# Phase tables of an S4 convolution: step tiles without doubled values, mode pairs written 128 bytes apart

## The chip, the cores and the metric

The kernel runs on one core of a Trainium2 chip. The core has five engines with queues of their own: TensorE (PE in the profile; its weight loads are the row PEld), VectorE (DVE), ScalarE (ACT), GpSimd (POOL) and SyncE (SP), which here only issues transfers. The metric is the device time of one execution in microseconds (us). The kernel before took 761.42 us in the median of three runs (760.34 to 763.97).

## The reference

The input is layer-normalised, and two branches are added to it: an S4 layer (a long convolution whose kernel K is a sum over 256 complex modes for each of 448 channels) and a PEER layer (16 heads, each picks the best of 64 x 64 experts by two scores, and adds a weighted row of a table).

```python
xn = layernorm(x)
# S4: K[d,l] = Re sum_n C[d,n] * dt*B[d,n] * exp(dt*A[d,n] * l),  l = 0..2047
P = exp((dt * A)[:, :, None] * l)
K = einsum("dn,dnl,dn->dl", C, P, dt * B).real
y = irfft(rfft(pad(xn)) * rfft(pad(K)))[:2048] + xn * Dskip
# PEER: q = xn @ w_q; s1, s2 = q1 . k1, q2 . k2; one expert per head
e = argmax(s1) * 64 + argmax(s2)
out = sum_h softmax(top) * gelu(xn . u[e]) * v[e]
result = x + y + out
```

The softmax is over one value.

## The kernel before, in words

**Convolution.** The 448 channels are cut into 56 batches of 8 (`batch`), two batches form a pair. A batch has R = 32 modes per partition (2 halves `h` of M = 16, which is 2 blocks of 128 modes times 8 channels). The exponential is split into magnitude and phase. TensorE makes the logarithms of the magnitudes (L579, L581) and ScalarE their exponentials `mg` (L590, L592). The phases are 32-bit integers, a full turn being 2 to the power 32, so sums wrap by themselves. For each mode 32 multiples a = 0..31 of the phase are needed. VectorE builds them in the tile `ph` for both batches of a pair by doubling: a first row (L610), then four additions (L614), which each add a shifted step to all that is there and so double it. The shifted steps are in the tile `st`, made by `steps` once for four batches by two shifts (L547) from the loaded phases `tp` and the shift amounts `amt`.

ScalarE turns the phases of one batch into a table `CS` with a sine half and a cosine half: sine (L629), absolute value (L632), and a sine of pi/2 minus that (L635). `CS` is ordered by mode, and within a mode by a: a mode's 32 values are contiguous. VectorE multiplies it into the magnitudes (L660, L662, L664, L666), TensorE sums over modes (L682), and after a small correction (L690, L693) transforms (L702) and ScalarE writes the result to `VK` (L706). After every 16 batches (the last time 8) `conv` multiplies with the transformed input: TensorE L798 (in the last piece L762 and L779), VectorE L808 (last piece L786), TensorE L830 (last piece L825), ScalarE L837, and SyncE stores the tile (L842). `final` loads it again (L1149, with a constant, L1151), transforms (L1159), copies (L1163), and GpSimd's queue adds it to the output (L1167).

**How phases lie before.** In `ph` the innermost index x (0 or 1) is the lowest bit of a. So two consecutive a of a mode are adjacent, 8 bytes. To add a step to both, `st` holds every step twice. ScalarE reads pairs: two values, then a jump of 512 bytes to the next pair. It writes `CS` without a gap.

**Scores and experts.** TensorE makes the scores (L961, L970), VectorE and ScalarE reduce them (L985 to L1006), and the indices go through memory. For the experts GpSimd's queue gathers rows (L1083), VectorE multiplies and sums each with the input (L1091), small steps on ScalarE and VectorE follow (L1098 to L1114), TensorE adds the weighted rows (L1121), ScalarE copies them (L1133), GpSimd's queue adds them to the output (L1136).

**Order.** Nothing is scheduled on the chip. `Plan` holds 72 streams of steps (`s4_ph` builds phases, `s4_act` the tables, `st_v` the shifted steps, `e_d` the experts' products and so on), and the string `ORDER`, one character a step, says whose next step is issued. Each engine executes its instructions in that order and waits by semaphores. The costs given with the steps in the code serve a planner outside and change nothing in the issued program.

Of the kernel before, what the change touches and what calls it, by code (L numbers as in the profile page):

```python
# [25 lines left out]
M = 2 * NB  # L26
# [89 lines left out]
class Plan:  # L116
# [57 lines left out]
    "4HH4HH44441444Z4444H606HH414144114H72III2II72II2I2I7728I8I2IJJ22I2I2I2I72KIZ414I82852I24K4I4COP224C4234LMLDHMHHH4LMDCLM4"  # L174
    "D3EC4EC6D44EI7II7IJJKKCLFDECMFDDEFF77877I47CI7I999FD9EEL44I7CCE8MFD8FDI749x48EI4F87CEC57IDD4N4FFRCRE9I47I79ZL4CFEFDR4EA4"
    "D7CF4MZ4xIENC979F8D8LIDEQ7SFI7M6EN7SRFARR7SOPSRQAA99JZSZAAGcGcSRSTRRSSRROdPSSRaBHUUUUxSUSSTUUUUUUUUUVWWeRRHXNYSSSaRYRRgS"
    "HbyyQfSOHyPRSLRSTyJhMRhgLhhgfRhhMffIfyhUzSSUzIUyGzRURSxz!S#!hUhI#yIzS$IyyQyO$Ih%ySiPcSTzyzUzURhzUyhy!##HURIU!HzI$U$zUR%S"
    "zUIygU!#ISh!h#yyyISRzKRVROizWx$W$%yyfziHHhNgxSfSzxPxKLISiz!#JM#RjRLRSfI!$$%QzIhhgTJfiIziGISSzMfykI!#yIyU#RUi&hRhh!yI$S$i"
    "dIeRXUSzUO%jhSIUNSlizIIhPkhLRhQzISMLhTMyRdiLzibURe!yyRzMfUzlyUiU##NY!U$$%LShSgJRjyRZZSifMhKhgHzz!UzKxiHfSfaN#Ufyy(LJ!Skh"
    "M#$hOPgUzxUiSL$%RRSyhhyymzxHTMhmlizxUUSRhhhn!nhHjhkhgLMURiUSLhhUyz#gRyRQV1iziSIiNI!fiIzz!ifSYclmISfhM#fQ$I$%hnSSgO#IyTWf"  # L180
    "IiUzjhiKZPhHI!&hRmUIhR#QkW$UhnI$UyyyyUzIzlzU%!hHjRy#z!iziS#Iy$RS$hkJyyyL%ZiUSzzHHdMhyRyLMelIbROzISz!I#!Iy#$SygiPfIhiSSXm"
    "zfzhRJmRUfRU$%L!nITnjhgfi#SIUIfMLhIhMkUIUiSgRRR#h!ISli$$N%OIJjKxcNJhzxyyVhhcyyxSzzSyUySUxzSzh!TPi#h!h#QmULUWZ$aih&Kyyhnf"
    "$UfURfU%MRziSzUgyzyLhNMhRgifSLfRQz!hSiH(yhg#HWzz#h!$R$hhbjZzz%Riyh!k#y!#MHYO$SSd$%iyHPIhekSizIIUSzlliIiRRLjhIKQghTzIUiSh"
    "UIR!#UihISMkhKyIyyfI!UI#URlmyS$I$fURfSShnJVY%NcgROhKxhfSajXxUizzyyPiSxzgLkhyymRQixzz!M#z#N!$Rhym$lhzfinyL&%RTSyzy(njUSUz"
    "hUz!yhhgzhzMU#Uhk!!SWR##il$$fh!Ri%R#hzhJfyi$yzfyxz$OzyfgxSxxS%KfimSiSiUhhP!gL#RMRhjhL#TiUiyUWSd!z$hRUSyzRMR$yy%yhkhSiyhS"
    "izUnjzhkilSROUNY(Qzlh!zhSzUPy&#!y#ymiSR$z$egyUb%hny!h#!aRyzTizfzUgzSfyyRURSXfiUR#$NQSU$UROzUihSSxoz!xYhgmzSf%yzSyP#h#Uy!"
    "h!hyfURRjnhTiRkhhS$U#hyS$y%UiymjUzilk!#UlxV$$xg%&hzzz!zzWh#!(Sn#hRSyyzyiz!iyyRmRS#V#$Wh!my$$inno$fUoyfigSSph%hzfgp%zfzUq"
    "rzqzyyphYj!hhzUrizfiyTkqpqroz#rhhhi#!!dpjqlW#$hrebiUh#kst$!hpg%pqWhxh$iorfoo$qltUxpgypyfzrhqxhciXfUg%irszijhUyifq&pzfrUi"
    "yhkhyyxy(zlzU!thozy#p#!qzz$hy$pjq!hr##iy!z$cay%yhhiyg$yUzfyUhzfqhrzhkpz%qr!pyyygUVzrtWihhuqppl#zfzyghrfi#!hy!ms(#fd#$yqm"
    "hyu!hr$%nqteth$ii$irnyiymjYbxxmhxsihnkxKnhjii%tzhWilgfhhYt&ykzgzzQffzzzz!yhhgh#if#yy!l$fmmh!$#h#!izz%iji$ynhyyuhnhyzkhhl"  # L190
    "z$zzihjgfhzi!hf#z!kayfli#gfifib$ih!hg$mhhuhijd%#hi)heh)(ym!nini#*ki$ljhxzXm%i+hhkf$xzxlxngh%hmgyyyizzifi&f!ynhhjgyy#yyhh"
    "i!khflf#zh$h*$y+hjmnkhca%hzziiilmnYyzg!hiz#y!hhzzyf#$zjgh$chzfykg%yh!zfzfifihdhzl#!hmi#i!eh##nh)o*+jb$i$!i$hg$ihk,%%ix)x"
# [12 lines left out]
class Kernel:  # L205
# [22 lines left out]
    def alloc(s):  # L228
# [1002 lines left out]
```

## Time and profile before

| | |
|---|---|
| median of three runs | 761.42 us |
| the profiled execution, its own time | 763.02 us |
| its span from first to last instruction | 761.1 us |
| VectorE busy | 669.5 us, 88% |
| TensorE busy | 652.1 us, 86% |
| ScalarE busy | 552.9 us, 73% |
| GpSimd busy | 360.7 us, 47% |
| mean granted TensorE clock | 0.915 |

The profile is one execution. A page gives each engine's busy time, a strip of 40 equal slices (a digit is the busy share in tenths) and groups of instructions: line, engine, operation, output and input tile, shape, count, busy time and mean length, then the idle time of the engine ahead of them and what ended it. Other views of the same trace cut it into stretches, list who waited for whom, and follow the chain of work that ended last.

### The profile page before, as it was taken

The numbers are of one execution on the slowest core, as the hardware profiler recorded it, in microseconds if no ns is written. First come the engines' busy times: TensorE is split into PE (matmuls) and PEld (weight loads), VectorE is DVE, ScalarE is ACT, GpSimd is POOL, SyncE is SP. The second block draws the span as 40 slices with busy tenths as digits, with TensorE's granted clock in tenths as the row PEclk, the third lists the DMA queues.
The fourth block names the chain that finished last, engine by engine and source line by source line (L and its number), as shares of the span: only waits on it lengthen the run. The fifth ranks groups of instructions, "written<-read, shape, count | busy, mean of one in ns | idle before, by whom it ended". The sixth has DMA issues, their size and how long they took to land.

```text
span 761.1 us, 19861 instructions
## 1 busy us (share of the span) xinstructions
PE 652.1 (86%) x7628; PEld 355.8 (47%) x7628; DVE 669.5 (88%) x1691; ACT 552.9 (73%) x1137; POOL 360.7 (47%) x307
## 2 busy tenths in 40 slices
PE   1999999999999999999887958679996587899882
PEld 0344333443444444444465734346763344576751
DVE  4896578999999999999999999999998999999840
ACT  3886147566876886774796898888898888999630
POOL 2011024544363645655447686484564657752523
PEclk9999999999999999999999877688987756999995
DMA  9998656978687896887989999899898999977998
GB/s 324 328 374 305 228 136 254 355 238 246 221 257 266 252 327 191 309 255 257 337 300 340 281 324 361 263 327 279 265 342 271 308 325 286 339 248 209 296 178 128
DMA packets 119095, 211.83 MB, mean 278 GB/s; under 512 B 38937, under 2 KB 94233, under 8 KB 118937
## 3 DMA queue, kind: packets, MB, share of 16 engines
q0 software_dynamic: 31232, 124.80, 51.6%
q1 hardware_dynamic: 87768, 85.77, 35.2%
q8 instruction: 60, 0.98, 0.5%
q14 instruction: 35, 0.28, 0.1%
HBM read 180.90 MB, written 33.29 MB: 281 GB/s over the span
## 4 chain that ended last, share of the span: by engine, by line
PE 41%; DVE 29%; ACT 14%; DMA 7%; issue 6%; SPq 1%; POOL 1%; POOLq 0%; DVEq 0%; ACTq 0%
PE sc L961 14%; DVE ue L1091 6%; PE U L798 3%; PE po L1121 3%; DVE mg L666 3%; DVE zi L662 3%; DVE ph L614 3%; PE kp L682 3%; PE sc L970 3%; DMA ue<-in_uv_dram,ig 3%; PE ip L830 2%; PE wc L862 2%; PE up L724 2%; ACT CS L629 2%; DMA VU<-vu_d 2%
## 5 line engine op out<-in xcount | busy, mean ns | idle before, releaser
L1083 POOL DMA_INDIRECT ue<-in_uv_dram,ig x256 | 312.6, 1221 | 309.0 <-PE po L1121 72.9
L961 PE MATMUL sc<-W,xt 128*128 128x512 f32 x384 | 180.1, 608 | 2.2 <-ACT xt L946 1.9
L1091 DVE SCALAR_TENSOR_TENSOR ue<-ue,xr 128x448 f32<-128x448 f32 x256 | 154.1, 617 | 4.0 <-DMA ue<-in_uv_dram,ig 4.0
L961 PEld LDWEIGHTS sc<-W,xt 128*128 128x128 f32 x384 | 69.7, 191 | 91.9 <-issue 83.9
L1121 PE MATMUL po<-ue,A 128*32 128x448 f32 x512 | 68.6, 616 | 9.4 <-DVE A L1114 5.0
L590 ACT ACTIVATE mg<-lg 128x512 f32<-128x512 f32 x112 | 63.4, 600 | 11.1 <-PE lg L579 10.6
L682 PE MATMUL kp<-mg 128*32 128x64 f32 x1792 | 62.3, 237 | 7.9 <-DVE kt L693 3.1
L666 DVE TENSOR_TENSOR mg<-mg,CS 128x1024 f32<-128x1024 f32 x56 | 68.2, 1217 | 0.0
L662 DVE TENSOR_TENSOR zi<-mg,CS 128x1024 f32<-128x1024 f32 x56 | 68.2, 1217 | 0.0
L635 ACT ACTIVATE CS<-CS,halfpi 128x1024 f32<-128x1024 f32 x56 | 64.5, 1152 | 0.8
L614 DVE CUSTOM_DVE_ANT_0 ph<-st,ph 128x512 uint16<-128x512 uint16 (+2 forms) x84 | 64.9, 772 | 0.2
L629 ACT ACTIVATE CS<-ph 128x1024 f32<-128x1024 int32 x56 | 62.6, 1118 | 1.4 <-issue 0.5
L632 ACT ACTIVATE CS<-ph 128x1024 f32<-128x1024 int32 x56 | 63.2, 1128 | 0.0
L682 PE MATMUL kp<-zi 128*32 128x64 f32 x1792 | 61.6, 234 | 0.0
L682 PEld LDWEIGHTS kp<-mg 128*32 128x32 f32 x1792 | 45.2, 119 | 29.2 <-issue 11.7
L579 PE MATMUL lg<-lc,rt 32*128 32x512 f32 x112 | 39.8, 548 | 21.5 <-ACT mg L590 17.5
L702 PE MATMUL vp<-f,kt 128*64 128x128 f32 x448 | 43.6, 326 | 16.5 <-ACT tl L1163 5.0
L985 DVE TENSOR_REDUCE mx<-sc 128x8 f32<-128x512 f32 x64 | 43.6, 682 | 14.6 <-PE sc L970 9.2
L682 PEld LDWEIGHTS kp<-zi 128*32 128x32 f32 x1792 | 47.2, 121 | 0.1
L798 PE MATMUL U<-VU,g 128*64 128x128 f32 x384 | 42.3, 301 | 5.4 <-DVE cp L808 2.7
L702 PEld LDWEIGHTS vp<-f,kt 128*64 128x64 f32 x448 | 28.9, 160 | 38.3 <-issue 11.9
L862 PE MATMUL wc<-wq,kk 128*64 128x448 f32 x128 | 31.7, 586 | 17.1 <-DMA wq<-in_wq_dram 17.1
(244 smaller groups left out, 1242.2 us busy)
## 6 DMA issues: line engine op xcount, KB each, us to landing
wq<-in_wq_dram SPq DMA_DIRECT2D x32, 448.0 KB
xr<-xn_d SPq DMA_DIRECT2D x64, 224.0 KB
vu_d<-vst SPq DMA_DIRECT2D x64, 112.0 KB
VU<-vu_d SPq DMA_DIRECT2D x12, 512.0 KB
t_d<-tq SPq DMA_DIRECT2D x24, 256.0 KB
tl<-t_d SPq DMA_DIRECT2D x12, 512.0 KB
ue<-in_uv_dram,ig POOLq DMA_INDIRECT x256, 6.4
xx<-in_x_dram SPq DMA_DIRECT2D x16, 224.0 KB
```

The costliest lines, as they stand in the source:

```text
L614: s.nc.vector.tensor_tensor(out=rw(n, 2 * n), in0=rw(0, n), in1=o["st"][:, k, b0:b0 + 2].rearrange("p b h m x -> p (b h m x)")[:, None].to ...
L629: s.nc.scalar.activation(CS[:, 1].rearrange("p (m r x) -> p m r x", r=16, x=2), four(s.ph), AF.Sin, scale=SC)
L635: s.nc.scalar.activation(B["CS"][:, 0], B["CS"][:, 0], AF.Sin, scale=-SC, bias=s.halfpi)
L662: V.tensor_tensor(out=zi[:, 512:], in0=mg[:, 512:], in1=CS[:, 1], op=ALU.mult)
L666: V.tensor_tensor(out=mg[:, 512:], in0=mg[:, 512:], in1=CS[:, 0], op=ALU.mult)
L682: s.nc.tensor.matmul(kp[32 * c:32 * c + 32, 64 * gi:64 * gi + 64], T[ri][:, 1024 + m:1056 + m], view(T[ri], m, [[512, 2], [1, 32]]), start ...
L702: s.nc.tensor.matmul(vp[64 * ri:64 * ri + 64, 128 * gi:128 * gi + 128], B["kt"][:, 64 * gi:64 * gi + 64], s.f1[:, ri], start=True, stop=True)
L798: s.nc.tensor.matmul(U[64 * h:64 * h + 64, sl, ri], s.g[q][:, 2 * kk + h, ri], src[:, k1 + h, :w], start=True, stop=True)
L961: s.nc.tensor.matmul(B["sc", q].rearrange("p a b -> p (a b)"), B["xt"][:, i], w, start=(q % 2 == 0 and i == 0), stop=(q % 2 == 1 and i == 2))
L1083: s.nc.gpsimd.indirect_dma_start(out=ue, out_offset=None, in_=s.io["uv"], in_offset=bass.IndirectOffsetOnAxis(ap=s.IDX[t][:, c, g:g + 1].b ...
L1091: s.nc.vector.scalar_tensor_tensor(Q["ue", c][:, :D], Q["ue", c][:, :D], 1.0, B["xr", c], op0=ALU.mult, op1=ALU.mult, accum_out=Q["dot"][: ...
L1121: s.nc.tensor.matmul(B["po"][32 * c:32 * c + 32, :D], Q["A"][:, c], Q["ue", c][:, D:], start=(g == 0), stop=(g == 3))
```

## The change

Three things change.

1. `st` holds each step once: the two shifts write 256 values a partition each and not 512. `amt` is transposed to suit.
2. In `ph` x now stands outside batch, half and mode, so that two adjacent values are two modes of one a. The first row is copied by x and no longer by h, each of its two instructions writing 64 contiguous values; the four additions have the sizes they had, and the added step row of 64 values is repeated 2, 4, 8 and 16 times in place of a row of 128 repeated 1, 2, 4 and 8 times. ScalarE's L629 and L632 read pairs of modes, with a jump of 256 bytes from pair to pair, and write the two modes of a pair 128 bytes (32 values) apart. `CS` holds the same values in the same places as before, so nothing behind it changes.
3. `ORDER` is a new string of the same steps. As many instructions of each kind are issued as before, with two exceptions: ScalarE's table loads are 64 in place of 62, and the shapes named above. The lines behind `steps` lie 1 to 4 lower in the file (L786 before is L782 after, L1091 is L1087).

```diff
 ORDER = (
-    "4HH4HH44441444Z4444H606HH414144114H72III2II72II2I2I7728I8I2IJJ22I2I2I2I72KIZ414I82852I24K4I4COP224C4234LMLDHMHHH4LMDCLM4"
...
+    "4HH4HH4474441464447I22II26442242I42IIC2447I1I4DI44012IC2I4I781HHJ414OECDC85FHH2JD8P274E8E4FLID7IIMF7IC2D22I4I44IECLCMID7"
...
-        s.amt = c.tile([128, 2, 4], I32, name="amt")
-        s.ph = c.tile([128, 16, 2, 2, M, 2], I32, name="ph")
+        s.amt = c.tile([128, 4, 2], I32, name="amt")
+        s.ph = c.tile([128, 16, 2, 2, 2 * M], I32, name="ph")
...
-            o["st"] = s.sm.tile([128, 4, 4, 2, M, 2], I32, name="st", bufs=s.o["ST"])
+            o["st"] = s.sm.tile([128, 4, 4, 2, M], I32, name="st", bufs=s.o["ST"])
             for h in range(2):
-                a = s.amt[:, h]
-                s.nc.vector.tensor_tensor(out=view(o["st"], 2 * M * h, [[16 * M, 4], [4 * M, 4], [1, 2 * M]]),
-                                          in0=view(o["tp"][:, 0, 0], 0, [[0, 4], [1, 4 * M], [0, 2]]),
-                                          in1=view(a, 0, [[1, 4], [0, 8 * M]]), op=ALU.logical_shift_left)
+                s.nc.vector.tensor_tensor(out=o["st"][:, :, :, h], in0=view(o["tp"][:, 0, 0], 0, [[0, 4], [M, 4], [1, M]]),
+                                          in1=view(s.amt, h, [[2, 4], [0, 4], [0, M]]), op=ALU.logical_shift_left)
...
                 if k < 0:
-                    for h in range(2):
-                        s.nc.vector.tensor_scalar(s.ph[:, 0, :, h].rearrange("p b m x -> p x b m"), o["tp"][:, :, h, b0:b0 + 2], 0, None,
-                                                  op0=ALU.logical_shift_left)
+                    for x in range(2):
+                        s.nc.vector.tensor_scalar(s.ph[:, 0, x].rearrange("p b (h m) -> p b h m", h=2), o["tp"][:, x, :, b0:b0 + 2].rearrange("p h b m -> p b h m"),
+                                                  0, None, op0=ALU.logical_shift_left)
                 else:
-                    n = 1 << k
-                    s.nc.vector.tensor_tensor(out=rw(n, 2 * n), in0=rw(0, n),
-                                              in1=o["st"][:, k, b0:b0 + 2].rearrange("p b h m x -> p (b h m x)")[:, None].to_broadcast([128, n, 4 * R]),
-                                              op=ALU.add)
+                    n = 2 << k
+                    s.nc.vector.tensor_tensor(out=ph[:, n:2 * n], in0=ph[:, :n],
+                                              in1=o["st"][:, k, b0:b0 + 2].rearrange("p b h m -> p (b h m)")[:, None].to_broadcast([128, n, 2 * R]), op=ALU.add)
...
         def four(v):
-            return view(v.rearrange("p r b h m x -> p (r b h m x)"), 2 * R * (b % 2), [[2, R], [4 * R, 16], [1, 2]])
+            return view(v.rearrange("p r x b m -> p (r x b m)"), R * (b % 2), [[2, M], [2 * R, 32], [1, 2]])
...
-            s.nc.scalar.activation(CS[:, 1].rearrange("p (m r x) -> p m r x", r=16, x=2), four(s.ph), AF.Sin, scale=SC)
+            s.nc.scalar.activation(CS[:, 1].rearrange("p (m c a) -> p m a c", a=32, c=2), four(s.ph), AF.Sin, scale=SC)
...
-            s.nc.scalar.activation(B["CS"][:, 0].rearrange("p (m r x) -> p m r x", r=16, x=2), four(s.ph), AF.Abs)
+            s.nc.scalar.activation(B["CS"][:, 0].rearrange("p (m c a) -> p m a c", a=32, c=2), four(s.ph), AF.Abs)
```

**What the new string does at three places.** The first is the end of VectorE's list, from the last product of the convolution on (`cp`, L786 before). `ue,dot` is an expert's product, `x`, `dw` and `th` are small steps of 4 values a partition, `A` the weights for TensorE. Before:

```order
L786 TENSOR_TENSOR cp<-us_8718,U 128x512
L1101 SCALAR_TENSOR_TENSOR x_8912<-x_8912,dot 128x4
L1114 TENSOR_TENSOR A<-mask,th 128x128
L1110 TENSOR_TENSOR dw<-dot,ig 128x4
L1107 SCALAR_TENSOR_TENSOR th<-th,dw 128x4
L1114 TENSOR_TENSOR A<-mask,th 128x128
```

Now, from the last `cp` (the third of a row of three) on:

```order
L782 TENSOR_TENSOR cp<-us_8694,U 128x512 x3
L1097 SCALAR_TENSOR_TENSOR x_8768<-x_8768,dot 128x4
L1103 SCALAR_TENSOR_TENSOR th<-th,dw 128x4
L1106 TENSOR_TENSOR dw<-dot,ig 128x4
L1110 TENSOR_TENSOR A<-mask,th 128x128
L1087 SCALAR_TENSOR_TENSOR ue,dot<-ue,xr 128x448
L1103 SCALAR_TENSOR_TENSOR th<-th,dw 128x4
L1087 SCALAR_TENSOR_TENSOR ue,dot<-ue,xr 128x448
L1110 TENSOR_TENSOR A<-mask,th 128x128
L1087 SCALAR_TENSOR_TENSOR ue,dot<-ue,xr 128x448 x2
L1097 SCALAR_TENSOR_TENSOR x_8978<-x_8978,dot 128x4
L1106 TENSOR_TENSOR dw<-dot,ig 128x4
```

after which a `th` and an `A` end the list. Four expert products that stood ahead of the convolution's last product now stand behind it.

The second place is TensorE's list at the same point. `ip` is the convolution's last transform (L825), `po<-ue,A` adds expert rows, `po<-tl,hl` is the work of `final`. Before:

```order
L825 MATMUL ip<-cp,e 128x256 x8
L1121 MATMUL po<-ue,A 32x448 x4
L825 MATMUL ip<-cp,e 128x256 x8
L1159 MATMUL po_8995<-tl,hl 32x128 x16
L1121 MATMUL po<-ue,A 32x448 x8
L1159 MATMUL po_9043<-tl,hl 32x128 x16
```

Now:

```order
L821 MATMUL ip<-cp,e 128x256 x8
L1155 MATMUL po_8983<-tl,hl 32x128 x16
L1117 MATMUL po<-ue,A 32x448 x12
L1155 MATMUL po_9039<-tl,hl 32x128 x16
L1155 MATMUL po_9066<-tl,hl 32x64 x16
```

The last transform no longer has expert rows ahead of it; all three remaining groups of them come behind.

The third place is ScalarE's list at the second and third pair of tables, where the two additional table loads are. Now (`exg` is an exponential for the experts, `th` a tanh):

```order
L1037 ACT_TABLE_LOAD
L1037 ACTIVATE exg<-top 128x32
L992 ACTIVATE eq<-sc,mx 128x64 x8
L723 ACTIVATE vst<-up 128x448
L686 ACTIVATE kt<-kp 128x2x63
L1094 ACTIVATE x_1210<-dot 128x4
L921 ACTIVATE xx<-xx,q,y 128x448
L625 ACT_TABLE_LOAD
L625 ACTIVATE CS<-ph 128x16x32x2
L1100 ACT_TABLE_LOAD
L1100 ACTIVATE th<-x_1210 128x4
L628 ACTIVATE CS<-ph 128x16x32x2
```

Before, the comparable stretch had one load ahead of both tables of a pair:

```order
L639 ACT_TABLE_LOAD
L639 ACTIVATE dum<-one 128x1
L1098 ACTIVATE x_948<-dot 128x4
L1104 ACTIVATE th<-x_948 128x4
L629 ACTIVATE CS<-ph 128x1024
L632 ACTIVATE CS<-ph 128x1024
L635 ACTIVATE CS<-CS,halfpi 128x1024
L946 ACTIVATE xt<-xtp 128x512
```

The exponential and the tanh now stand between the steps of a pair's tables and bring loads of their own.

More of the change, by code (lines that the diff above doesn't have):

```diff
@@ L178 @@
[L178 to L189, printed above, removed]
@@ L205 @@
+    "stt!#!$#)u$z$*z,+%,uu$z)%z!##!$$%&+(*,+))*)*)++**,,++,,,")
 class Kernel:
@@ L287, in sets @@
                 for k in range(4):
-                    s.nc.gpsimd.memset(s.amt[:, h, k:k + 1], k + 2 + 6 * h)
+                    s.nc.gpsimd.memset(s.amt[:, k, h:h + 1], k + 2 + 6 * h)
         x0 = s.amt_done = p.add("c_g", "POOL", 1600, sets)
@@ L543, in sh @@
         def sh():
[L544 removed]
+            o["st"] = s.sm.tile([128, 4, 4, 2, M], I32, name="st", bufs=s.o["ST"])
             for h in range(2):
[L546 to L549 removed]
+                s.nc.vector.tensor_tensor(out=o["st"][:, :, :, h], in0=view(o["tp"][:, 0, 0], 0, [[0, 4], [M, 4], [1, M]]),
+                                          in1=view(s.amt, h, [[2, 4], [0, 4], [0, M]]), op=ALU.logical_shift_left)
         x = p.add("st_ld", "SP", xf(512, 256), l, deps=s.tp_done, take=("tpl",))
[L551 removed]
+        o["ready"] = [p.add("st_v", "DVE", dv(512), sh, n=1, deps=[x, s.amt_done], take=("st",))]
         return o
```

47 lines of the change are left out of this document (28 added, 19 removed).

## The prediction

> **What bounds the kernel now.** I read the page's busy shares first, then the same cut into stretches, then who VectorE waits for, then the rows of the edited lines, and last the chain at the end.
>
> ```profile
> PE 652.1 (86%) x7628; PEld 355.8 (47%) x7628; DVE 669.5 (88%) x1691; ACT 552.9 (73%) x1137; POOL 360.7 (47%) x307
> core 0: us, PE busy (x) PEld busy (x) DVE busy (x) ACT busy (x) POOL busy (x), PEclk, DMA share, GB/s
> 0.00:375.00 375.00, 349.53 (x2270) 148.18 (x2270) 331.26 (x838) 247.44 (x571) 147.47 (x136) 1.00 0.81 274
> 375.00:700.00 325.00, 262.49 (x4428) 176.98 (x4430) 310.82 (x782) 281.89 (x513) 189.29 (x153) 0.84 0.94 299
> 700.00:730.00 30.00, 27.47 (x690) 22.27 (x684) 26.62 (x70) 18.34 (x43) 14.11 (x11) 1.00 0.78 222
> 730.00:761.00 31.00, 12.59 (x248) 8.36 (x246) 0.75 (x5) 5.23 (x13) 9.86 (x8) 0.68 0.99 174
> ```
>
> The cut at 375 us is where the scores end. Until then TensorE is the fullest engine (349.5 of 375 us). From 375 to 700 it is VectorE: 310.8 of 325 us, 96%; ScalarE follows with 281.9, that is with 43.1 us idle. From 730 on VectorE has nothing left and a tail of 31 us runs through transfers. So a microsecond less on VectorE behind 375 us should come off the end, while ScalarE has some room, but not much.
>
> ```profile
> DVE x L1101 <- ACT x L1098: 4.6, 6, 2.7
> DVE th L1107 <- ACT th L1104: 3.8, 5, 1.3
> ...
> DVE ue L1091 <- DMA ue<-in_uv_dram,ig: 2.0, 2, 1.0
> ...
> DVE zi L660 <- ACT CS L629: 1.3, 1, 1.3
> ```
>
> These are VectorE's waits from 150 to 730 us (total, times, longest). None is large; the tables (`CS`) hold it up once, for 1.3 us, and gathered rows twice, for 2.0 us. VectorE is bound by its own work there.
>
> **The change part by part.** The sum is made on the profiled execution: a span of 761.1 us, a time of 763.02, which is 1.6 us above the median of 761.42.
>
> *The shifted steps.* 28 instructions shrink from 512 to 256 values.
>
> ```profile
> L547 DVE TENSOR_TENSOR st<-tpl,amt 128x512 int32<-128x512 int32 x28 | 18.0, 682 | 0.0
> L666 DVE TENSOR_TENSOR mg<-mg,CS 128x1024 f32<-128x1024 f32 x56 | 68.2, 1217 | 0.0
> L664 DVE TENSOR_TENSOR mg<-mg,CS 128x512 f32<-128x512 f32 x56 | 38.3, 683 | 0.0
> 0.00:150.00 150.00, 1.28 (x2) 1.00 0.82 289
> 150.00:375.00 225.00, 5.13 (x8) 0.99 0.80 264
> 375.00:700.00 325.00, 11.56 (x18) 0.84 0.94 299
> ```
>
> The last three rows are L547 alone, by stretch (VectorE busy, count). VectorE's other two-input products take 683 ns for 512 values and 1217 for 1024, so 534 ns per 512, and L547's 682 stands on the same line. 256 values then take 682 - 267 = 415 ns, and one instruction saves 0.267 us; all 28 save 7.5 us of VectorE time. The two that run before 150 us save nothing, since VectorE has room there. The eight up to 375 us lie beside a TensorE that stays as full as it was; the 18 behind it lie where VectorE is the bound. So between 18 x 0.267 = 4.8 and 26 x 0.267 = 6.9 us. I take 4.8, because in the first stretch TensorE's row is the fuller one.
>
> *First row and additions of `ph`.*
>
> ```profile
> L610 DVE TENSOR_SCALAR ph<-tpl 128x64 int32<-128x64 int32 x56 | 8.6, 209 | 0.4 <-ACT CS L632 0.3
> L614 DVE CUSTOM_DVE_ANT_0 ph<-ph,st 128x256 uint16<-128x256 uint16 x28 | 7.9, 282 | 0.0
> L614 DVE CUSTOM_DVE_ANT_0 ph<-st,ph 128x512 uint16<-128x512 uint16 x28 | 11.7, 418 | 0.1
> L614 DVE CUSTOM_DVE_ANT_0 ph<-st,ph 128x2048 uint16<-128x2048 uint16 x28 | 34.0, 1215 | 0.0
> L1107 DVE SCALAR_TENSOR_TENSOR th<-th,dw 128x4 f32<-128x4 f32 x64 | 9.9, 154 | 5.0 <-ACT th L1104 4.1
> ```
>
> The four additions keep their sizes. Only the repetition of the step row doubles, and today the forms that repeat it once, twice and eight times lie on one line: (418 - 282) / 256 = 0.53 ns a value, (1215 - 418) / 1536 = 0.52. Repetition is free, so 0. The first row's 56 instructions keep 64 values and only write them without gaps; they could gain at most what separates 209 ns from the 154 of an instruction on 4 values, 3.1 us in all, or lose as much. I take 0, since the count of values is the same.
>
> *ScalarE's tables.* 112 instructions (L629, L632) read pairs as before and now write one value here and the next 128 bytes on.
>
> ```profile
> L629 ACT ACTIVATE CS<-ph 128x1024 f32<-128x1024 int32 x56 | 62.6, 1118 | 1.4 <-issue 0.5 <-DVE ph L614 0.4 <-DVE mg L666 0.2
> L632 ACT ACTIVATE CS<-ph 128x1024 f32<-128x1024 int32 x56 | 63.2, 1128 | 0.0
> L446 ACT ACTIVATE pv<-pw 128x896 f32<-128x896 f32 x1 | 1.0, 951 | 2.3 <-issue 2.3
> L592 ACT ACTIVATE mg<-lg 128x512 f32<-128x512 f32 x56 | 31.9, 597 | 15.2 <-PE lg L581 15.1
> L706 ACT ACTIVATE VK<-vp 128x256 f32<-128x256 f32 x56 | 21.5, 387 | 13.4 <-PE vp L702 13.3
> L803 ACT ACTIVATE us<-U 128x256 f32<-128x256 f32 x48 | 18.3, 388 | 6.7 <-PE U L798 5.9 <-DVE cp L808 0.8
> 375.00:700.00 325.00, 40.50 (x36) 0.84 0.94 299
> ```
>
> No row shows such a write; this is the large unknown. ScalarE's step per value is (597 - 388) / 256 = 0.82 ns. Two rows show it jumping on the reading side. L706 reads every value 128 bytes from the last, out of PSUM, and takes 387 ns where L803, of the same size, reads without jumps in 388. And L446's 951 ns for 896 contiguous values would be 951 + 128 x 0.82 = 1056 for 1024, so jumping after every pair costs L629 and L632 some 62 to 72 ns. From below the cost is therefore 0. From above I let every value take a second step: 1024 x 0.82 = 0.84 us an instruction, 94 us in all, of which 72 instructions (the last row is L632 alone, 36 of them; L629 has as many) or 60 us fall between 375 and 700 us. I take 0, by L706, the nearest row in distance and in engine; the upper end is a rival.
>
> The Trainium skill, "Advanced Engine Details and Errata", section "SBUF Cachelines", speaks against that choice: SBUF is in lines of 16 bytes, at least two hits on a line are needed to hide the access, and a different line on each access is penalised. The trace agrees with it as far as pairs go and has no row for SBUF writes; it does not say whether a write counts. By the rule the sum would be that of the first rival; by L706's row it stays as taken here.
>
> *Two table loads more.*
>
> ```profile
> L639 ACT ACT_TABLE_LOAD x28 | 35.9, 1283 | 0.4
> ```
>
> 2 x 1.283 = 2.6 us on ScalarE, at the second and third pair of tables, thus well before 375 us, where ScalarE is busy 247 of 375 us. That idle time hides it; 0 (or 2.6 if those tables were waited for).
>
> *The end of the order.*
>
> ```profile
> 729.27 0.68 DVE L786 TENSOR_TENSOR cp<-us,U 128x512 f32<-128x512 f32 x1
> 729.88 1.98 PE ip L825 x16
> 736.01 4.91 DMA t_d<-tq
> 741.06 2.89 DMA tl<-t_d
> 755.99 1.31 POOLq L1227
> L1091 DVE SCALAR_TENSOR_TENSOR ue<-ue,xr 128x448 f32<-128x448 f32 x256 | 154.1, 617 | 4.0 <-DMA ue<-in_uv_dram,ig 4.0
> L1091 DVE DVE_READ_ACCUMULATOR ue<-ue,xr 128x1 f32 x256 | 20.3, 79 | 0.0
> L1114 DVE TENSOR_TENSOR A<-mask,th 128x128 f32<-128x128 f32 x64 | 18.3, 287 | 2.7 <-PE po L1121 2.0
> ```
>
> The chain at the end hangs on the convolution's last product `cp`: transform, store, load, and the output, 31.1 us from its end (729.95) to 761.1. Behind it VectorE has three small steps and two `A`: 3 x 0.154 + 2 x 0.287 = 1.0 us. In the new order it has four expert products (4 x 0.696), three `A` and seven small steps: 2.8 + 0.9 + 1.1 = 4.7 us. With as much VectorE work in all, `cp` ends 3.7 us sooner against it, and the chain with it. TensorE's last `ip` has no expert rows ahead of it any more, so nothing there takes this back; the last experts are late next, 3.7 us further behind `cp`, and end in one output transfer that still comes before `final`'s. I take -3.7; the other end is 0, if the last expert rows hold the chain.
>
> Elsewhere the string only exchanges work between times when the engines are full; I put that at 0, between 5 us less (VectorE's waits above hold little more) and 5 more.
>
> Sum: -4.8 - 3.7 = -8.5 us, that is 754.5 against the profiled execution and 752.9 against the median: **753 us**. A measurement of this kernel can tell about 0.5%, 3.8 us, from no change.
>
> **The rivals.**
>
> First, *scattered writes cost ScalarE a second step*. The skill's rule above would give this. Place: L629 and L632 from 375 to 700 us. It decides from the point where ScalarE there becomes fuller than VectorE: 310.8 - 4.8 = 306 against 281.9 leaves 24 us, over 72 instructions 0.33 us each, so at a length of about 1.45 us. At 1118 + 840 = 1960 ns ScalarE would have 281.9 + 60 = 342 us of work in a stretch of 325: 17 us longer if it never waited, 31 us longer at VectorE's 96%. VectorE's saving is then worth nothing, and the end gives 3.7 back: 761.4 + 13 to 27, some 774 to 789, 782 in the middle. For it speaks that reading by pairs is not quite free today; against it L706.
>
> Second, *the saving does not reach the end*: transfers carry 0.94 of what the 16 engines can between 375 and 700 us, and a faster VectorE asks for gathered rows sooner. Then L1091's wait of 2.0 us grows by the 4.8 us saved, and if the last experts also hold the tail the time stays at 761. Against it: that wait is short today.
>
> Third, *the new start is slower*: the first shifted steps wait for the phases to go to memory and back. At the end a store took 4.9 and a load 2.9 us, together 7.8, and the stretch behind the last parameter step has less VectorE work in it than before. A stall there holds the scores' reductions behind it on VectorE, then TensorE. It decides where the stall is longer than the 8.5 us gained; one of 13 us would give 761.4 - 8.5 + 13 = 766. The first tables stand at about the same place among TensorE's scores, which speaks against it.
>
> **How the numbers follow.** The forecast, faster than 757.6, gets 0.43, with a range of its own of 747 to 757 (the three unknown ends: 2.1 more of the steps, 3.1 of the first row, 5 of the string). No change within 3.8 us gets 0.12, mostly the second rival. Scattered writes get 0.33. The new string being slower with free writes, 765 to 772, gets 0.12. So faster 0.43, same 0.12, slower 0.45. The range from 747 to 790 leaves out about 0.07 below and 0.1 above.
>
> **What would show it.** Right: the steps at 415 ns; L625 and L628 near 1.12 us; VectorE still at 95% or more behind 375 us; about 31 us from the end of the last `cp` to the end of the span, with some 4 us of VectorE work beside it. Wrong: L625 and L628 above 1.45 us, ScalarE's strip at 9 and VectorE waiting for `CS`; or VectorE's waits for gathered rows grown to 5 us and more; or an idle VectorE ahead of the first shifted steps.

## The result and the profile after

The changed kernel took 853.68 us in the median of four runs (851.64 to 855.85), beside 762.69 (760.34 to 765.49) for the kernel before in four: 1.119 times as long, with an interval of 1.114 to 1.124. The forecast was 753, and 790 at most.

The page of the changed kernel (engines; VectorE's and ScalarE's strips; the chain by engine):

```profile
PE 683.6 (80%) x7628; PEld 372.5 (44%) x7628; DVE 664.6 (78%) x1691; ACT 651.5 (76%) x1139; POOL 347.2 (41%) x307
DVE  5566988996888898998888777778887778888740
ACT  2757377878768868748877899998889999999821
ACT 45%; PE 31%; DVE 12%; issue 5%; DMA 4%; SPq 1%; POOL 1%; POOLq 0%; ACTq 0%; DVEq 0%
```

ScalarE has 651.5 us of work in place of 552.9, and its strip stands at 8 and 9 through most of the second half. VectorE fell from 88% to 78% of the span. The chain, which before was 41% TensorE, 29% VectorE and 14% ScalarE, now runs through ScalarE for 45%. The groups of the edited lines (output and input, count, busy us, mean ns, idle time ahead):

```profile
L546 DVE TENSOR_TENSOR st<-tpl,amt 128x256 int32<-128x256 int32 x28 | 10.6, 418 | 0.0
L607 DVE TENSOR_SCALAR ph<-tpl 128x64 int32<-128x64 int32 x56 | 8.9, 206 | 19.6 <-ACT CS L628 17.8 <-ACT th L1100 1.7
L611 DVE CUSTOM_DVE_ANT_0 ph<-st,ph 128x2048 uint16<-128x2048 uint16 x28 | 34.1, 1218 | 0.1
L628 ACT ACTIVATE CS<-ph 128x1024 f32<-128x1024 int32 x56 | 115.6, 2065 | 0.0
L625 ACT ACTIVATE CS<-ph 128x1024 f32<-128x1024 int32 x56 | 115.4, 2060 | 0.0
```

VectorE's part came out as worked out: steps at 418 ns, first row and additions unchanged. But L625 and L628, the writes 128 bytes apart, take 2060 and 2065 ns where L629 and L632 took 1118 and 1128. That is 0.94 us more on each of 112 instructions, 105 us in all. (Records of successive instructions overlap by 0.1 to 0.2 us, so busy time grew by less, 98.6 us, the two table loads included.) ScalarE has no idle time ahead of them (the last column): it is the others that wait. VectorE's waits after (us in total, times, longest):

```profile
DVE x L1097 <- ACT x L1094: 27.0, 17, 7.3
DVE kt L689 <- ACT kt L686: 24.3, 13, 3.6
DVE th L1103 <- ACT th L1100: 21.5, 19, 3.3
DVE ph L607 <- ACT CS L628: 17.8, 9, 3.2
```

Only one of the four is a wait for a table's instruction, L628 releasing the single `ph` tile. The other three are waits for ScalarE's short steps, of 4 or 126 values. During the 24.3 us of waits for `kt`, ScalarE spent 15.8 on L625 and L628; one such place is shown below. For `x` and `th` these two lines cover only 5.3 of 27.0 and 3.7 of 21.5 us; the rest of those waits has other causes. The longest wait for `x`, 7.3 us, begins behind the convolution's last product, and the kernels with short tables have one like it there (8.1 and 8.3 us). The cut at the last scores, of the changed kernel:

```profile
0.00:405.10 405.10, 356.73 (x2269) 150.58 (x2270) 326.76 (x829) 281.65 (x570) 144.54 (x134) 0.97 0.77 253
405.10:853.90 448.80, 326.83 (x5360) 221.93 (x5358) 337.81 (x863) 369.85 (x569) 202.68 (x173) 0.80 0.83 244
```

The scores end 30 us later than before, at 405.1 in place of 375, and what follows takes 63 us more. In neither part is ScalarE full: 281.7 of 405.1 us, then 369.9 of 448.8 (fourth busy number).

One thing about the chips is needed to read the runs below: the kernel before took 762 to 766 us on some chips and 827 to 842 on others, so kernels are compared in microseconds only within one series of runs on one chip, and ratios are to the kernel before in the same series.

### The profile page after: what moved, and what is told of

Read it like the earlier page. It is cut to its first block, busy times and chain, and to the rows that moved or that the text cites. A ratio compares the mean times of both kernels' runs of the same rounds, so it can differ in the third digit from the quotient of the medians.

```text
span 853.9 us, 19867 instructions
## 1 busy us (share of the span) xinstructions
PE 683.6 (80%) x7628; PEld 372.5 (44%) x7628; DVE 664.6 (78%) x1691; ACT 651.5 (76%) x1139; POOL 347.2 (41%) x307
## 4 chain that ended last, share of the span: by engine, by line
ACT 45%; PE 31%; DVE 12%; issue 5%; DMA 4%; SPq 1%; POOL 1%; POOLq 0%; ACTq 0%; DVEq 0%
ACT CS L625 10%; ACT CS L628 10%; PE sc L957 8%; PE ip L826 4%; ACT CS L631 4%; PE kp L678 3%; ACT L635 3%; PE po L1117 3%; DVE ue L1087 2%; PE lg L577 2%; ACT mg L588 2%; ACT mg L590 2%; ACT eq L992 2%; PE U L794 2%; PE vp L698 1%
## 5 line engine op out<-in xcount | busy, mean ns | idle before, releaser
L1079 POOL DMA_INDIRECT ue<-in_uv_dram,ig x256 | 298.8, 1167 | 365.0 <-PE po L1117 183.1
L957 PE MATMUL sc<-W,xt 128*128 128x512 f32 x384 | 184.6, 620 | 8.1 <-ACT xt L942 7.6
L1087 DVE SCALAR_TENSOR_TENSOR ue<-ue,xr 128x448 f32<-128x448 f32 x256 | 154.8, 617 | 1.1 <-DMA xr<-xn_d 1.1
L628 ACT ACTIVATE CS<-ph 128x1024 f32<-128x1024 int32 x56 | 115.6, 2065 | 0.0
L625 ACT ACTIVATE CS<-ph 128x1024 f32<-128x1024 int32 x56 | 115.4, 2060 | 0.0
L577 PE MATMUL lg<-lc,rt 32*128 32x512 f32 x112 | 44.3, 586 | 45.0 <-ACT VK L702 17.6
L678 PE MATMUL kp<-mg 128*32 128x64 f32 x1792 | 67.7, 247 | 8.5 <-DVE mg L662 3.3
L611 DVE CUSTOM_DVE_ANT_0 ph<-st,ph 128x256 uint16<-128x256 uint16 (+1 forms) x112 | 73.0, 652 | 0.4
L678 PE MATMUL kp<-zi 128*32 128x64 f32 x1792 | 67.2, 245 | 0.2 <-issue 0.2
L826 PE MATMUL ip<-cp,e 64*128 64x256 f32 x384 | 54.9, 439 | 3.2 <-ACT tq L833 2.1
L577 PEld LDWEIGHTS lg<-lc,rt 32*128 32x128 f32 x112 | 17.3, 213 | 80.7 <-ACT mg L588 24.4
L698 PEld LDWEIGHTS vp<-f,kt 128*64 128x64 f32 x448 | 29.3, 162 | 48.8 <-DVE kt L689 19.9
L826 PEld LDWEIGHTS ip<-cp,e 64*128 64x128 f32 x384 | 43.4, 221 | 13.7 <-issue 2.6
```

Of the source, the lines that this page charges most:

```text
L577: s.nc.tensor.matmul(ps, ro["rt"][rs, i], s.lc[rs, :512], start=True, stop=True)
L625: s.nc.scalar.activation(CS[:, 1].rearrange("p (m c a) -> p m a c", a=32, c=2), four(s.ph), AF.Sin, scale=SC)
L628: s.nc.scalar.activation(B["CS"][:, 0].rearrange("p (m c a) -> p m a c", a=32, c=2), four(s.ph), AF.Abs)
L678: s.nc.tensor.matmul(kp[32 * c:32 * c + 32, 64 * gi:64 * gi + 64], T[ri][:, 1024 + m:1056 + m], view(T[ri], m, [[512, 2], [1, 32]]), start ...
L698: s.nc.tensor.matmul(vp[64 * ri:64 * ri + 64, 128 * gi:128 * gi + 128], B["kt"][:, 64 * gi:64 * gi + 64], s.f1[:, ri], start=True, stop=True)
L826: s.nc.tensor.matmul(Q["ip", h][:, 2 * w * x:2 * w * x + 2 * w], s.e[r, k], Q["c", x][r, :, ab, ri], start=(i == 0), stop=(i == 3))
```

## The experiments

### On a slower chip: the parts alone

Kernel before: 836.92 us (824.97 to 849.07). Theory W: the scattered writes carry the loss. Rivals: reading does (R), or the new order does (O). The forecasts in microseconds were made for a chip like the first; here the ratios are read in their place.

**Writes in a row, all else as changed.** Values land in wrong places of `CS`.

```diff
-            s.nc.scalar.activation(CS[:, 1].rearrange("p (m c a) -> p m a c", a=32, c=2), four(s.ph), AF.Sin, scale=SC)
+            s.nc.scalar.activation(CS[:, 1].rearrange("p (m a c) -> p m a c", a=32, c=2), four(s.ph), AF.Sin, scale=SC)
```

and the same on L628.

> The changed kernel, but L625 and L628 write their 1024 values in the order in which they read them, without gaps. (The tables then hold the values of a mode pair in the wrong places, so the convolution's result is wrong; the work is the same.) Theory W, the scattered write is the whole cost: both lines fall from 2.06 us to about 1.12, and the kernel to 748 to 760 us. Rival R, the reading of mode pairs 256 bytes apart costs it: both lines stay at 2.06 us, the kernel at about 854.

855.6 us, ratio 1.026 (1.019 to 1.033); L625 at 1114 ns, ScalarE busy 557.4 us. Reading pairs of modes costs nothing; R falls. But 1.026 is not below 1, so something else costs too.

**New order, old layout.** Only `ORDER` is replaced in the kernel before.

> The kernel before with nothing changed but the order string. Theory W: the string is worth little by itself, 752 to 772 us. Rival O, the new string is what makes the kernel slow, since it puts steps where they wait: above 790 us.

853.22 us, ratio 1.021 (1.014 to 1.029), between the two forecasts. The order has a price of its own.

**New layout, old order.** The changed kernel with the string of before.

> The changed kernel with the order string of before. Theory W: as slow as the changed kernel, 840 to 865 us, L625 and L628 at 2.06 us. Rival O: the old string keeps most of the loss away, below 800 us, the lines at 2.06 us all the same.

902.03 us, ratio 1.080 (1.069 to 1.091). The layout is the larger part with the old order too. O as the whole cause falls.

**Half the dose.** The change of the first experiment on L628 only, so that only the sine (L625) is scattered.

> The changed kernel, but only the sine half (L625) is written scattered, the absolute values (L628) without gaps, so half the dose. (The tables' absolute values lie in the wrong places, so the convolution's result is wrong.) If each microsecond of ScalarE goes through to the end from the first on: half of the 92 us lost, about 800 us. If ScalarE's idle time of 43 us between 375 and 700 us first takes up what it can: less than half, 765 to 785 us.

876.04 us, ratio 1.053 (1.044 to 1.063): 20.4 us above the run with both in a row, for 46.3 us more of ScalarE (603.7 against 557.4). The forecasts left out the order's price, so they are not decided by this. The same kernel on another slower chip (828.92 us for the kernel before):

> The changed kernel with the sine's writes scattered and the absolute value's in a row, its values in wrong places: half of the 105 us of added ScalarE time. On the slower chip it had 1.053, 20 us above the run with both in a row. If each added microsecond of ScalarE counts the same, it stands halfway between the interleaved kernel (1.020) and the changed one (1.120): 1.06 to 1.08. If ScalarE's idle time takes the first part, as the prediction's rival had it (some 40 us free between 375 and 700 us): 1.02 to 1.045. If the first part does the harm: above 1.09.

870.66 us, 1.054 (1.045 to 1.062), between the two forecasts.

### On a chip like the first

Kernel before: 765.74 us (762.22 to 769.45).

**The kernel before, for its profile here,** as a baseline for the slower chip's pauses (last section).

> The kernel before, unchanged, for its own profile on the chip of this call. In the runs so far the new order with the old layout stood at 1.021 of the kernel before, on a chip where the kernel before itself took 837 us and not 762; in that profile TensorE was idle 44.4 us before L682 in 101 pieces that no semaphore ended, and in the profile of before on the first chip it was idle there by 7.9 us with none of that kind. Theory C (the pauses belong to the chip): on a chip with 820 us or more this profile shows 30 to 50 us of such pauses before L682; on a chip near 762 us it shows less than 3. Theory O (the new order makes them): less than 3 us on either chip.

A span of 758.8 us, last scores at 375.6, no pauses before L682 without a releaser. On this chip both theories forecast that, so it does not choose between them.

**The changed kernel again.**

> The changed kernel, on the same chip as the other runs of this call. Theory W (ScalarE's doubled writes carry the loss, and small steps wait behind them): ratio to the kernel before 1.10 to 1.13 on a chip near 762 us; on a chip with 820 us or more TensorE's own pauses lie partly in the time in which it waits for ScalarE anyway, ratio 1.06 to 1.10. Theory O (the new order carries it, 1.02 or more by itself and the rest by chance of the chip): the ratio follows that of the order alone and stays under 1.05 on the slower chip.

855.69 us, ratio 1.120 (1.114 to 1.126).

**The two modes of a pair written side by side.** ScalarE writes in a row, the magnitudes' constant gets the same column order, and TensorE picks a mode's 32 columns at every second value. The two activations are edited as in the first experiment, and:

```diff
-                lc[:, kind, c, 256 * half + 32 * c + a] = bj[32 * half + a]
+                lc[:, kind, c, 256 * half + 64 * (c // 2) + c % 2 + 2 * a] = bj[32 * half + a]
...
-                            m = 32 * (NB * t + 4 * gi + c)
-                            s.nc.tensor.matmul(kp[32 * c:32 * c + 32, 64 * gi:64 * gi + 64], T[ri][:, 1024 + m:1056 + m],
-                                               view(T[ri], m, [[512, 2], [1, 32]]), start=(n == 0), stop=(n == 3))
+                            m = 32 * (NB * t + 4 * gi + c - c % 2) + c % 2
+                            s.nc.tensor.matmul(kp[32 * c:32 * c + 32, 64 * gi:64 * gi + 64], view(T[ri], 1024 + m, [[2, 32]]),
+                                               view(T[ri], m, [[512, 2], [2, 32]]), start=(n == 0), stop=(n == 3))
```

> The changed kernel with the two modes of a pair written side by side, so that ScalarE writes 1024 values in a row; the constant for the magnitudes has its columns in the same order, and TensorE picks a mode's 32 columns at every second value (L678). It computes the whole result. Theory W: L625 and L628 at 1.11 to 1.13 us, ScalarE busy about 557 us, ratio to the kernel before 0.99 to 1.03 (the contiguous run had 1.026, with values in wrong places). Rival P (TensorE pays for reading every second value): L678 above 270 ns instead of 245, 3584 of them, ratio 1.05 to 1.15. Rival R (reading costs ScalarE, not writing): L625 stays near 2.06 us.

781.2 us, ratio 1.020 (1.014 to 1.026): 74.5 us less than the changed kernel on the same chip. The groups of this kernel:

```profile
L628 ACT ACTIVATE CS<-ph 128x1024 f32<-128x1024 int32 x56 | 63.3, 1131 | 0.0
L625 ACT ACTIVATE CS<-ph 128x1024 f32<-128x1024 int32 x56 | 63.1, 1127 | 0.4 <-DVE ph L611 0.3
L678 PE MATMUL kp<-mg 128*32 128x64 f32 x1792 | 67.6, 243 | 7.7 <-DVE mg L662 3.8 <-ACT mg L590 1.2 <-ACT tl L1159 0.7
L678 PE MATMUL kp<-zi 128*32 128x64 f32 x1792 | 66.4, 240 | 0.0
```

TensorE pays a little for reading every second value. The changed kernel had 244 ns here, but its granted clock was lower (0.886 against 0.924). The order alone (last part of this section) had 0.920 on a chip like this one and reads without gaps:

```profile
L682 PE MATMUL kp<-mg 128*32 128x64 f32 x1792 | 63.8, 239 | 12.0 <-DVE mg L666 6.6
L682 PE MATMUL kp<-zi 128*32 128x64 f32 x1792 | 63.0, 237 | 0.0
```

That is 3 to 4 ns less a product; with overlaps taken out, the `kp` products keep TensorE busy for 70.9 us there and 75.0 here. So P has some 4 us of TensorE time, far from its 1.05 to 1.15, and the 74.5 us may be a little less than what the scattered writes cost.

Why do 94.5 us of ScalarE (651.4 against 556.9 busy) cost 74.5? The cut at the last scores, first of the interleaved kernel, then of the changed one on the same chip:

```profile
0.00:383.00 383.00, 348.62 (x2270) 148.57 (x2270) 323.38 (x826) 250.80 (x570) 143.29 (x134) 1.00 0.80 263
383.00:778.00 395.00, 306.64 (x5360) 210.28 (x5358) 336.99 (x866) 306.12 (x569) 214.26 (x174) 0.85 0.94 281
```

```profile
0.00:405.80 405.80, 357.82 (x2269) 152.12 (x2270) 327.37 (x833) 281.82 (x570) 142.30 (x134) 0.97 0.77 253
405.80:850.00 444.20, 323.50 (x5360) 219.62 (x5358) 336.85 (x859) 369.58 (x569) 208.58 (x173) 0.81 0.84 246
```

Up to the last scores ScalarE gets 31.0 us more work, and the stretch grows by 22.8. Behind them it gets 63.5 more, and what is left of the span grows by 48.8 (444.4 in place of 395.6). So about three quarters of each added microsecond reach the end, although ScalarE is busy only 69% of the first stretch and 83% of the second. Its idle time behind the scores fell only from 89 to 75 us: it is not room for more work, but time in which it waits for VectorE or TensorE, which wait for it in turn. One such place in the changed kernel, ScalarE's instructions from 639.75 us (start, length):

```profile
639.75 0.19 ACT L1094 ACTIVATE x<-dot 128x4 f32<-128x4 f32 x1
639.85 1.96 ACT L625 ACTIVATE CS<-ph 128x1024 f32<-128x1024 int32 x1
641.62 1.97 ACT L628 ACTIVATE CS<-ph 128x1024 f32<-128x1024 int32 x1
643.39 0.30 ACT L686 ACTIVATE kt<-kp 128x126 f32<-128x126 f32 x1
```

VectorE at that time (in brackets its idle time and what ended it):

```profile
639.97 0.16 DVE L1097 SCALAR_TENSOR_TENSOR x<-x,dot 128x4 f32<-128x4 f32 x1 [0.47 <-ACT x L1094]
643.72 0.16 DVE L689 TENSOR_TENSOR kt<-kp,dsk 128x2 f32<-128x2 f32 x1 [3.58 <-ACT kt L686]
```

and TensorE:

```profile
636.24 0.32 PE L678 MATMUL kp<-zi 128*32 128x64 f32 x8
638.43 0.92 PE L698 MATMUL vp<-f,kt 128*64 128x128 f32 x8 [1.87 <-DVE kt L689]
643.94 0.84 PE L577 MATMUL lg<-lc,rt 32*128 32x512 f32 x2 [4.59 <-DVE kt L689]
```

TensorE's products `kp` have long been there. But the 0.30 us copy L686 stands behind two table instructions (L625, L628) of another batch in ScalarE's queue. VectorE waits 3.58 us for it, ahead of all its expert work, and TensorE 4.59 us for VectorE. With short tables the same rank in the queue costs less: VectorE's wait for L686 is 22.5 us in all in the changed kernel and 11.1 in the interleaved one, the wait at L607 17.9 against 2.6.

**The jump moved to the reads.** ScalarE writes in a row and reads each value 256 bytes behind the last.

```diff
-            return view(v.rearrange("p r x b m -> p (r x b m)"), R * (b % 2), [[2, M], [2 * R, 32], [1, 2]])
+            return view(v.rearrange("p r x b m -> p (r x b m)"), R * (b % 2), [[2, M], [1, 2], [2 * R, 32]])
...
-            s.nc.scalar.activation(CS[:, 1].rearrange("p (m c a) -> p m a c", a=32, c=2), four(s.ph), AF.Sin, scale=SC)
+            s.nc.scalar.activation(CS[:, 1].rearrange("p (m c a) -> p m c a", a=32, c=2), four(s.ph), AF.Sin, scale=SC)
```

> The changed kernel with the jump moved from ScalarE's writes to its reads: it writes 1024 values in a row and reads each value 256 bytes behind the one before, where the change read two by two. It computes the whole result with TensorE's reads as they were. Theory W1 (only writes pay): L625 and L628 at 1.11 to 1.20 us, ratio to the kernel before 0.99 to 1.03. Theory W2 (a jump costs on either side): L625 at 1.9 to 2.1 us, and the time of the changed kernel, within 1%.

857.62 us, ratio 1.123 (1.117 to 1.128), L625 at 2016 ns. A jump costs on either side (W2), and the time is that of the changed kernel: what counts is ScalarE's length, however it comes about.

### The price of a jump by itself

Copies of 1024 values on ScalarE, four times each, behind the kernel before; for example

```diff
+            s.nc.scalar.activation(view(b, 0, [[1, 2], [2, 512]]), view(a, 0, [[1, 1024]]), AF.Copy)
```

which writes 8 bytes apart.

> The kernel before, and behind its end four rounds of copies of 1024 values (512 where PSUM takes part) on ScalarE, and of multiply-adds on VectorE: in a row, then with the writes or the reads jumping by 8, 16, 32, 64 and 128 bytes, in the change's own pattern (two streams 128 bytes apart, written in turn), and by pairs of neighbours; and the same 128-byte jump on a read from PSUM and on a write to PSUM. Only the durations of these lines count. Theory L (the SBUF is reached by short lines, two values in the same line keep the pace): 8 bytes and pairs of neighbours near the row's own 1.1 us on ScalarE, 16 bytes and all above near 2.0 us, alike for reads and writes; from PSUM no difference, 0.6 us in both forms, as L706 reads it. Theory D (the doubling grows with the jump): a step between each two sizes. Theory V (it is ScalarE alone): VectorE's lines stay within 5% of its row.

ScalarE, lengths min/median/max in ns. In a row; writes 8, 16, 32, 128 bytes apart; the change's pattern; writes by pairs; reads 8, 16 and 128 bytes apart:

```profile
L1215 ACT ACTIVATE pb<-pa x4: 1047/1056/1056, 825.0 to 963.1; 128x1024 f32<-128x1024 f32 x4
...
L1216 ACT ACTIVATE pb<-pa x4: 1115/1116/1117, 826.0 to 964.2; 128x1024 f32<-128x1024 f32 x4
...
L1217 ACT ACTIVATE pb<-pa x4: 1998/1998/1998, 827.2 to 965.3; 128x1024 f32<-128x1024 f32 x4
...
L1218 ACT ACTIVATE pb<-pa x4: 2032/2032/2033, 829.2 to 967.4; 128x1024 f32<-128x1024 f32 x4
...
L1220 ACT ACTIVATE pb<-pa x4: 1932/1932/1933, 833.2 to 971.4; 128x1024 f32<-128x1024 f32 x4
...
L1221 ACT ACTIVATE pb<-pa x4: 1970/1970/1972, 835.2 to 973.3; 128x1024 f32<-128x1024 f32 x4
...
L1222 ACT ACTIVATE pb<-pa x4: 1082/1082/1082, 837.2 to 975.3; 128x1024 f32<-128x1024 f32 x4
...
L1223 ACT ACTIVATE pb<-pa x4: 1118/1121/1121, 838.3 to 976.4; 128x1024 f32<-128x1024 f32 x4
...
L1224 ACT ACTIVATE pb<-pa x4: 2012/2012/2012, 839.5 to 977.6; 128x1024 f32<-128x1024 f32 x4
...
L1227 ACT ACTIVATE pb<-pa x4: 1936/1936/1936, 845.5 to 983.7; 128x1024 f32<-128x1024 f32 x4
```

The step lies between 8 and 16 bytes, on both sides: two values in 16 bytes keep the pace, one does not, and longer jumps change little (1917 to 2039 ns). Theory L holds for ScalarE, and D (growing with the jump) falls. From PSUM (512 values; in a row, then every value 128 bytes on), and the same jump read from SBUF:

```profile
L1245 ACT ACTIVATE pb<-pq x4: 597/597/597, 864.1 to 1002.2; 128x512 f32<-128x512 f32 x4
...
L1246 ACT ACTIVATE pb<-pq x4: 597/597/597, 864.7 to 1002.9; 128x512 f32<-128x512 f32 x4
...
L1249 ACT ACTIVATE pb<-pa x4: 1051/1051/1052, 866.5 to 1004.7; 128x512 f32<-128x512 f32 x4
```

A jump of 128 bytes in PSUM is free here; the same 512 values read from SBUF with that jump take 1051 ns.

### What is left: the new order

**The order alone, on a slower chip (828.92 us) and on a chip like the first.**

> The old layout with the new order, for its ratio beside the kernel before on a chip near 762 us (1.021 on the slower one). Theory W: 1.01 to 1.03, and the same within 1% as the changed kernel with its pairs written side by side (1.020): then the loss splits into some 2% of the order and some 10% of ScalarE's writes, and the half-width steps bring nothing that can be seen in this order. Rival: 0.99 to 1.01, the order is free, and the 2% of the interleaved kernel is TensorE's or VectorE's price of reading every second value.

848.79 us, ratio 1.022 (1.014 to 1.030).

> The old layout with the new order, for a chip on which the kernel before takes near 762 us (1.021, 1.022 and 1.015 on three slower ones). Theory W (the order costs some 2%, and nothing is left for the layout's other parts): 1.012 to 1.028. Rival (the order is free there, and the interleaved kernel's 1.020 is the price of reading every second value): 0.995 to 1.008.

785.1 us beside 763.48 (757.66 to 770.06): ratio 1.030 (1.025 to 1.035), so 21.6 us, just above W's range. The 2% of the interleaved kernel are thus, in the main, not the price of its layout. The profiled span is 778.6, 17.5 above the first profile of before, and splits by the same marks: last scores at 383.0 in place of 375.0 (8.0 us), from there to the end of the last `cp` 362.1 in place of 355.0 (7.1), and a tail of 33.5 in place of 31.2 (2.4):

```profile
L786 DVE TENSOR_TENSOR cp<-us,U x8: 676/678/687, 738.4 to 744.4; 128x512 f32<-128x512 f32 x8
```

The stretches of the order alone up to 200 us, then those of the kernel before:

```profile
0.00:150.00 150.00, 125.80 (x513) 51.88 (x514) 106.50 (x226) 87.45 (x211) 31.43 (x37) 1.00 0.78 269
150.00:200.00 50.00, 43.65 (x336) 18.21 (x338) 42.26 (x116) 36.78 (x83) 18.88 (x16) 1.00 0.78 243
```

```profile
0.00:150.00 150.00, 129.06 (x517) 51.91 (x518) 111.26 (x244) 86.26 (x217) 34.63 (x41) 1.00 0.82 289
150.00:200.00 50.00, 48.91 (x359) 21.32 (x358) 48.61 (x122) 36.53 (x78) 19.20 (x16) 1.00 0.80 260
```

At 200 us TensorE has done 8.5 us less (169.5 against 178.0), which is about the delay of the scores. Many short waits grow, most of them behind the scores: TensorE's at L702 for `kt` from 3.0 to 13.3 us, at L1121 for `A` from 5.0 to 13.9, both in the whole span. Which rows of the string make them was not tried.

**The interleaved layout with the old order,** on four slower chips. On the first the kernel before took 828.92 us.

> The pairs written side by side, with the old order: the half-width steps with neither the doubled writes nor the new order. It computes the whole result. Theory H (the prediction's term: 28 steps of 0.267 us less, 4.8 to 6.9 us of it before the last scores): 754 to 760 beside 762 to 766, ratio 0.988 to 0.995. Theory N (VectorE's saving goes into waits in its own order): 0.997 to 1.004. Theory P (reading every second value costs TensorE 5 ns on 3584 products, 18 us): 1.01 to 1.02.

836.69 us, ratio 1.014 (1.007 to 1.020), in P's range. The two later series with a ratio:

> Pairs written side by side with the old order, for a chip near 762 us (1.014 and 1.004 on two slower ones). Beside the interleaved kernel with the new order, 1.020 on the faster chip, it gives the price of the new order there. Theory H (the shifted steps' saving of 4.8 to 6.9 us reaches the end, the order costs 2.5 to 3%): 0.988 to 0.996. Theory N (the saving goes into waits, the order costs 2%): 0.997 to 1.005. Theory P (reading every second value costs, the order nothing): 1.012 to 1.025.

842.93 beside 838.9, ratio 1.001 (0.996 to 1.007), in N's.

> The interleaved layout with the old order, for a chip on which the kernel before takes near 762 us (on three slower ones 1.014, 1.004 and 1.001). Theory H: 0.988 to 0.996. Theory N: 0.997 to 1.005, and the new order's price is then some 2%. Theory P: 1.012 to 1.025.

834.37 beside 827.16, ratio 1.011 (1.006 to 1.017), between the two. One more series gives no ratio, since the kernel before spread from 825.36 to 855.99 (median 841.54); the order alone had 854.48 there, this kernel 845.08, the half dose 874.68:

> The old layout with the new order, once more, for a chip on which the kernel before takes near 762 us (on slower ones it had 1.021 and 1.022 of the kernel before). Theory W (the order costs 2%, the doubled writes the rest): 1.012 to 1.03, last scores near 383 us as in the interleaved kernel, and the same time as that kernel within 1%. Rival (the order is free there, and the interleaved kernel's 1.020 is the price of reading every second value): 0.995 to 1.008.

> Pairs written side by side with the old order, the whole result computed, for a chip near 762 us (1.014 on a slower one, where TensorE also pauses without a releaser before L678). Theory H (the shifted steps' saving of 4.8 to 6.9 us reaches the end): 0.988 to 0.996. Theory N (it goes into waits): 0.997 to 1.005. Theory P (TensorE's or VectorE's price for reading every second value): 1.008 to 1.02.

> The changed kernel with the sine's writes scattered and the absolute value's in a row (values in wrong places), for a chip near 762 us, where the interleaved kernel had 1.020 and the changed one 1.120. Each added microsecond of ScalarE counting alike: 1.06 to 1.08. ScalarE's idle time taking the first part: 1.02 to 1.05.

On the slower chips, then, no gain of the half-width steps can be seen; theory H did not show. But this kernel also pays TensorE's price (median product 223 ns, against 219 in the kernel before on the first of these chips), so the steps were not measured alone, and between N and P it stays open. On the faster chip this kernel has not run. No version here was shown to be faster than the kernel before.

## Why the prediction was wrong, point by point

On the faster chip, the change's 90.0 us (855.69 against 765.74) are 74.5 between scattered and side-by-side writes (measured, same chip) and 15.5 for the rest. The order alone costs 21.6 on such a chip by another series, which leaves some -6 for the layout's other parts, TensorE's 4 us of the interleaved kernel among them; the two intervals (1.014 to 1.026 with them, 1.025 to 1.035 without) just touch.

- *The shifted steps*: the length was right, 418 ns against 415, and 7.4 us of VectorE time went. Whether the 4.8 us taken reached the end is open: -6 would fit, but the two profiled spans are both 778.6 us, and the old order showed no gain on slower chips.
- *First row and additions*: right, 206 ns against 209 and 1218 against 1215.
- *ScalarE's tables*: this is the step that failed, "I take 0, by L706, the nearest row in distance and in engine". L706 reads PSUM, and a jump there is free, as the probe shows; SBUF is another memory. That row was no evidence on writes to SBUF. The rows that were evidence did not contain a jump after every single value: L629 and L446 only showed that pairs are nearly free. The upper end, one more step of 0.82 ns a value, was also short: it is 0.92 (942 ns / 1024). The rule weighed there, the Trainium skill's "Advanced Engine Details and Errata", section "SBUF Cachelines", pointed the right way: 1116 ns at 8 bytes and 1998 at 16 agree with lines of 16 bytes and two hits, for writes as for reads.
- *Two more table loads*: the order alone has them as well; they are inside its 21.6 us and were not measured apart.
- *The end of the order*: -3.7 was wrong. The last `cp` was to end 3.7 us sooner, with 31.1 us behind it as before. With the order alone it ends 15.1 us later (745.1 against 729.95), and 33.5 us follow; in the changed kernel 34.2. The step's premise, that VectorE's amount of work sets when `cp` ends, did not hold: between the last scores and the last `cp` VectorE is idle for 23.9 us in the order alone, against 17.6.
- *The rest of the string, 0 within 5*: mis-sized. Together with the end it is +21.6 us (19.3 to 26.8 by the interval).
- *First rival*: mechanism and sign were right, with 0.33, and the place as far as it went. Its price was not: 13 to 27 us, against 74.5. It let ScalarE's idle time take the work until the engine was fuller than VectorE; the runs show about three quarters of the added time arriving, with ScalarE 69% and 83% busy. It also left out the stretch before the last scores, where 22.8 us of the loss lie. Whether the first half of the dose is cheaper is open: on a slower chip it cost 20.4 us for 46.3 (0.44), and the full dose with this order was run only on the faster ones.
- *Second rival*: no transfer took anything back; they carry less after (0.83 behind the scores, against 0.94). *Third rival*: the order is slower, as it had it, but the first shifted steps had no idle time ahead of them; its place was wrong.

## What to carry to other kernels

Price an access pattern by the memory it goes to and by how many of its values, one after the other, share 16 bytes: rows of PSUM say nothing on SBUF, and pairs of values say nothing on single ones. On an engine that several others wait for by turns, idle time is not room: here about three quarters of the time added to ScalarE reached the end with the engine at 69 and 83%, in part because short steps queue behind the long ones, as shown for `kt`. (On a slower chip the half dose passed on 0.44 of what it added.) And a newly written order is a change with a price of its own, to be measured alone.

## What the hardware showed beyond that

Reads and writes differ where two streams 128 bytes apart alternate: written in turn they take 1970 ns (L1221 above), read in turn 1268, though no two successive values share 16 bytes in either.

```profile
L1228 ACT ACTIVATE pb<-pa x4: 1268/1268/1268, 847.5 to 985.6; 128x1024 f32<-128x1024 f32 x4
```

VectorE has a step at the same place, against theory V, but a smaller one: its multiply-add of 1024 values takes 695 ns with writes 8 bytes apart, as in a row, 1071 with 16 bytes and 1034 with 128.

```profile
L1231 DVE TENSOR_SCALAR pb<-pa x4: 695/695/696, 850.6 to 988.8; 128x1024 f32<-128x1024 f32 x4
...
L1232 DVE TENSOR_SCALAR pb<-pa x4: 1069/1071/1075, 851.3 to 989.5; 128x1024 f32<-128x1024 f32 x4
...
L1235 DVE TENSOR_SCALAR pb<-pa x4: 1033/1034/1035, 854.6 to 992.8; 128x1024 f32<-128x1024 f32 x4
```

On the slower chips the instructions looked at have much the same lengths (L682 219 ns in the median on both, L629 1108 and 1109 against 1107 and 1116), but TensorE pauses before the many short products L682 with no releaser that the profile shows. TensorE's waits in the kernel before with the probe behind it, up to the probe:

```profile
PE kp L682 <- issue: 24.6, 66, 0.5
```

On the faster chip the kernel before has none of these and the order alone 0.9 us, so they go with the chip and not with the new order. They are the largest of TensorE's waits there, but less than the 66 us between the chips; what else makes the difference, and what the pauses are, stays open.
